# Attention rows mixed by 32 x 32 products before the value weights, and three row sums taken with the scores

## The chip, the cores and the metric

The kernel runs on one core of a Trainium2 chip. Its engines are TensorE (PE in the profile; its weight loads are listed apart as PEld), VectorE (DVE), ScalarE (ACT), GpSimd (POOL) and SyncE (SP, which issues DMAs). Each engine works through its own instructions in order. The metric is the device time of one execution in microseconds; lower is better.

## The reference

A graph of 10000 nodes with 160000 edges is propagated seven times; each node then has eight tokens (its own row and seven hops), on which one attention block and a weighted readout run:

```python
    h = x
    toks = [x]
    for _ in range(K):
        msg = h[src] * deg_inv_sqrt[src, None] * deg_inv_sqrt[dst, None]
        h = _segment_sum(msg, dst, N)
        toks.append(h)
    tok = jnp.stack(toks, axis=1)                      # (N, K+1, D)
    t = _layernorm(tok, axis=-1)
    q   = jnp.einsum('nkd,de->nke', t, wq)
    key = jnp.einsum('nkd,de->nke', t, wk)
    v   = jnp.einsum('nkd,de->nke', t, wv)
    scale = 1.0 / (D ** 0.5)
    attn = _softmax(jnp.einsum('nkd,nld->nkl', q, key) * scale, axis=-1)
    o = jnp.einsum('nkl,nld->nkd', attn, v)
    o = tok + jnp.einsum('nkd,de->nke', o, wo)
    r = _layernorm(o, axis=-1)
    alpha = _softmax(jnp.einsum('nkd,d->nk', r, w_r), axis=-1)
    return jnp.einsum('nk,nkd->nd', alpha, o)
```

K is 7, D is 128, everything is f32.

## The kernel before

The hops (`class Hops`) take the time up to 3300 us and are not touched. The change is in `attention` and in the constants that `Attention.constants` prepares.

**Tiling.** A group is 16 nodes x 8 tokens = 128 rows of 128 numbers. There are 625 groups, dealt into 40 supergroups: the first has one group, the other 39 have `SG` = 16. Within a group the 128 rows lie on the partitions, and each block of 32 partitions holds four whole nodes, so attention never crosses a block of 32.

**The steps for supergroup i**, by name. `xT` transposes the groups on PE, four to a PSUM bank (a "quarter"), and ScalarE copies them out. `uT` multiplies by `M`, which folds query and key weights, the centring and the scale. `val` multiplies each group by `Wv`, 131 columns: 128 for the value and output weights together, and three that yield one number per row each (column 128 feeds `extras`, 129 is the readout weight's product with the row, 130 is the row's difference of mean and first element, used by `norms`). `score` makes the 32 x 32 blocks of products in 32-column tiles of the array, and `soft1a`, `soft1b`, `soft_exp`, `soft2` pick each row's own eight numbers out of its block and take the softmax. `soft3` transposes the weights in 32 x 32 blocks on VectorE (`t4`), and four GpSimd copies put the blocks on the diagonal of `PT`, a 128 x 128 matrix per group that is zero elsewhere. `attend` multiplies `PT` with the values; `resid` adds the input on VectorE. `squares` (ScalarE, one activation per group with an accumulated sum) and `stats` (VectorE) give the second moments of the input and of the output; `norms`, `root`, `norms2` turn them into scales. `read1` to `read3` and `store` are the readout. `same_node` spreads numbers among the rows of a node by a product with a constant matrix (`sm`).

**Order.** The order is written out by hand: the loop at the end of `attention` runs over i, and each turn emits, for several supergroups at once, `xT` of i + 1, `val`, `uT` and `score` of i, softmax of i - 1, `attend` and `resid` of i - 2, `stats` of i - 3, and the readout of i - 4 and i - 5, in four parts q = 0 to 3. No planner moves anything; every engine executes its instructions in the order of the text. The tag `a` has three PSUM banks shared by `xT`, `uT` and `val`; `attend` has two of its own, `score` one, `sm` one, the readout one.

**In the profile** an f32 product appears as two loads and two products. The names there are those of tiles: `pt` and `xT` for `xT`, `pu` and `uT` for `uT`, `pv` and `v` for `val`, `po` for `attend`, `ps` for `score`, `pT` for the diagonal copies, `junk` for `squares`, `pf` for `read3`, `tab` for the input and output rows.

## Time and profile before

| what | value |
|---|---|
| median of three runs | 3979.82 us (3978.59 to 3985.85) |
| the profiled execution | 3981.58 us |
| its span, first to last instruction | 3979.8 us |
| mean granted TensorE clock | 0.972 |
| PE busy over the span | 3701.6 us (93%) |
| VectorE busy | 3304.5 us (83%) |
| ScalarE busy | 2650.2 us (67%) |
| GpSimd busy | 1682.8 us (42%) |
| first `pt` of the attention stage | 3304.93 us |

Shares over the whole span mix the hops with the attention stage, whose limits are others; the stage is the last 17% of the time, and its own rows have to be read by stretches. A group's row gives line, engine, operation, tiles (out <- in), shapes and count, then busy time and mean duration in ns, then the engine's idle time just ahead of these instructions and what ended it. In the views in order of time a row gives start, length and count of a run of like instructions; the ends of matmuls are modelled, so the distance between two starts is the surer measure.

### The profile page before, as it was taken

Reading aid. Unit: us, or ns where it says so; the run is one execution under the profiler, and the core shown is the slowest. Engines: PE = TensorE matmul, PEld = TensorE weight load, DVE = VectorE, ACT = ScalarE, POOL = GpSimd, SP = SyncE. Lnnn points to the kernel's source line nnn. Section 1 sums busy time; section 2 is a strip of 40 time slices with the busy share of each in tenths; the row PEclk is TensorE's granted clock in tenths of the full one; section 3 lists DMA queues with packets and bytes.
Section 4 is the critical chain, followed back from the end, with each engine's and each line's share of the span. In section 5 each row is a group of like instructions: output and inputs, shape, how many; then the busy total and the mean of one; then the engine's idle time right before and its main releaser. Section 6 shows DMA issues by size and latency. Waiting matters only on the chain. (4 is left out here: it accounts for less than half of the span.)

```text
span 3979.8 us, 163459 instructions
## 1 busy us (share of the span) xinstructions
PE 3701.6 (93%) x69691; PEld 3036.0 (76%) x69691; DVE 3304.5 (83%) x6945; ACT 2650.2 (67%) x6799; POOL 1682.8 (42%) x1900
## 2 busy tenths in 40 slices
PE   5776899999989999999999999999999998999997
PEld 3765666666657888888888888888888887888875
DVE  8999999999976777777777777777776666999998
ACT  6674366666665666666666666666665558888884
POOL 0000333333335555555555555555555552222222
PEclk8898899999989999999999999999999999999998
DMA  3100354444456666666666666666666662222220
GB/s 109 28 1 1 121 158 149 145 156 148 151 171 195 200 201 197 204 202 201 195 202 202 195 203 203 200 195 204 202 189 206 189 187 73 74 74 79 79 75 13
DMA packets 320616, 594.82 MB, mean 149 GB/s; under 512 B 55623, under 2 KB 213541, under 8 KB 314629
## 3 DMA queue, kind: packets, MB, share of 16 engines
q1 hardware_dynamic: 220005, 478.41, 38.6%
q0 software_dynamic: 35392, 72.55, 6.1%
q10 hardware_dynamic: 64480, 33.33, 2.9%
q8 instruction: 546, 8.95, 1.0%
q14 instruction: 193, 1.58, 0.1%
HBM read 455.43 MB, written 128.67 MB: 147 GB/s over the span
## 5 line engine op out<-in xcount | busy, mean ns | idle before, releaser
L545 ACT CAST eb<-p 128x512 f16<-128x512 f32 x3081 | 1591.3, 603 | 675.8 <-PE p L542 648.5
L545 DVE CAST eb<-p 128x512 f16<-128x512 f32 x1896 | 1179.4, 683 | 345.5 <-PE p L542 331.2
L542 PE MATMUL p<-tab,w 128*32 128x256 f16 x39816 | 1285.4, 274 | 34.7 <-ACT eb L545 23.0
L518 PE MATMUL acc<-eb,w 128*128 128x256 f16 (+1 forms) x9954 | 1238.9, 273 | 12.3 <-DVE indeg L593 9.7
L542 PEld LDWEIGHTS <-w 128*32 128x32 fp8e4 x39816 | 1002.0, 97 | 234.6 <-issue 181.9
L489 POOL DMA_INDIRECT og<-tabh,oidx x553 | 632.7, 1144 | 1257.0 <-PE acc L504 656.7
L518 PEld LDWEIGHTS <-w 128*128 128x128 fp8e4 x9954 | 952.6, 98 | 180.9 <-issue 68.7
L489 POOL DMA_INDIRECT og<-tabd,oidx x541 | 559.3, 1034 | 447.0 <-PE acc L531 265.4
L571 POOL TENSOR_SCALAR r<-s,ctok 128x128 f32<-128x128 f32 x474 | 296.8, 626 | 27.3 <-DVE s L533 13.4
L675 ACT ACTIVATE tab<-s,c 128x128 f16<-128x128 f32 x395 | 158.5, 401 | 202.8 <-DVE s L533 202.8
L676 DVE SCALAR_TENSOR_TENSOR tab<-s,c,tab 128x128 f16<-128x128 f32 x395 | 139.9, 354 | 183.1 <-ACT tab L675 183.0
L318 ACT ACTIVATE o<-oh,d2s 128x79 f16<-128x79 f16 x800 | 204.6, 372 | 79.3 <-PE ta L332 79.3
L533 DVE TENSOR_REDUCE s<-acc 128x128 f32<-128x256 f32 x553 | 228.5, 413 | 23.3 <-PE acc L531 16.1
L938 ACT ACTIVATE junk<-tab 128x128 f32<-128x128 f32 x625 | 245.1, 394 | 0.0
L479 DVE TENSOR_TENSOR w<-dsl,iof 128x2432 fp8e4<-128x2432 f16 x79 | 211.7, 2680 | 0.0
L332 PE MATMUL ta<-o,ro 128*128 128x158 f16 x1250 | 122.2, 270 | 76.9 <-DVE ro L328 76.9
L924 PEld LDWEIGHTS po<-v,pT 128*128 128x128 f32 x1250 | 159.0, 193 | 43.6 <-issue 27.6
L332 PEld LDWEIGHTS <-ro 128*128 128x128 f16 x1250 | 116.9, 115 | 81.3 <-DVE ro L328 81.1
L913 PE MATMUL pv<-Wv,xT 128*128 128x131 f32 x1250 | 175.3, 282 | 2.9 <-ACT xT L893 1.8
L996 POOL TENSOR_TENSOR p<-e,in 128x512 f32<-128x512 f32 (+1 forms) x40 | 40.8, 1019 | 322.3 <-DVE e L994 311.3
L924 PE MATMUL po<-v,pT 128*128 128x128 f32 x1250 | 166.6, 277 | 7.0 <-DVE tab L930 5.4
L913 PEld LDWEIGHTS pv<-Wv,xT 128*128 128x128 f32 x1250 | 152.2, 190 | 19.6 <-issue 8.2
(275 smaller groups left out, 4492.0 us busy)
## 6 DMA issues: line engine op xcount, KB each, us to landing
w<-gsd SPq DMA_DIRECT2D x474, 592.0 KB
gsd<-w SPq DMA_DIRECT2D x79, 592.0 KB
rb<-srow SPq DMA_DIRECT2D x79, 576.0 KB
tok<-r SPq DMA_DIRECT2D x546, 64.0 KB
tab<-tok SPq DMA_DIRECT2D x273, 128.0 KB
tabd<-tab ACTq DMA_DIRECT2D x395, 64.0 KB
og<-tabh,oidx POOLq DMA_INDIRECT x553
og<-tabd,oidx POOLq DMA_INDIRECT x541
```

The source lines that it names most:

```text
L318: A.activation(o[:, j - a, NK:, i], oh[:, j, :, i], AF.Copy, scale=d2s[:, ch, c0:c0 + 1])
L332: T.matmul(ta, ro[:, j - a, :, i], o[:, j - a, :, i], start=j + i == 0, stop=j + i == NP)
L479: V.tensor_tensor(w[:, :NJ * 128].rearrange("p (j d) -> p j d", d=128), dsl[:, g, :, None].to_broadcast([128, NJ, 128]), self.iof1[:, None ...
L489: self.nc.gpsimd.indirect_dma_start(out=o, out_offset=None, in_=src[0] if i == NI else src[1], in_offset=bass.IndirectOffsetOnAxis(ap=self ...
L518: T.matmul(acc[0][:, :m], w[:, J * 128:(J + 1) * 128], e[:, j, :m], start=first and J == 0, stop=J == NG - 1 and not (first or late))
L533: V.tensor_reduce(s, acc[0][:, 0:256].rearrange("p (h d) -> p d h", h=2), axis=X, op=ALU.add)
L542: T.matmul(p[32 * q:32 * q + 32, j], w[:, NJ * 128 + s * CAP:NJ * 128 + (s + 1) * CAP], tab[:, s, :], start=True, stop=True)
L545: (A.copy if evac(jj) else V.tensor_copy)(e[:, :n, 0:256], p[:, :n].rearrange("p j h d -> p j (h d)"))
L571: self.nc.gpsimd.tensor_scalar(r, s, ct[:, t:t + 1], None, op0=ALU.mult)
L913: T.matmul(p[:, g - a, :], S[i]["xT"][:, g, :], Wv, start=True, stop=True)
L924: T.matmul(p[:, g - a, :], PT[i % 2][:, g, :], S[i]["v"][:, g, :128], start=True, stop=True)
L938: A.activation(j, S[i]["x"][:, g, :], AF.Square, bias=S[i]["x"][:, g, 0:1], scale=-1.0, accum_out=S[i]["sq"][:, g:g + 1])
```

## The change

The rows are now weighted before they meet the value weights. `mix` multiplies, for each group and each block of 32 partitions, the block of the input (as the loaded operand, 32 partitions x 128 columns) by the transposed 32 x 32 block of softmax weights, in row tiles of the array, with one PSUM bank for each of the four blocks; four ScalarE copies bring the result, already transposed, to `yT`. `attend` then multiplies `yT` by `Wv`. `val`, its copies, `PT` and the GpSimd copies are gone. `score` changes sides: `xT` is loaded and `U` is streamed, which holds for each block of 32 columns of `uT` three columns of `Wv` behind it; the three numbers per row come out with the scores (64 numbers apart, two PSUM banks), and `sums` copies them. For the last two groups of a supergroup the second moments of the input come from VectorE (`xstats`, `NQ` = 14) in place of ScalarE, in one tile with those of the output. One PSUM tag of five banks serves `xT`, `uT`, `mix`, `attend` and `read3`. The order is written anew as one list.

```diff
-        T.matmul(pw[:, 0:128], wT[:, 0, :], wT[:, 1, :], start=True, stop=True)
+        T.matmul(pw[:, 0:128], wT[:, 1, :], wT[:, 0, :], start=True, stop=True)
...
+    U = cp.tile([128, SG, 4, 35], F32, name="U")
+    V.tensor_copy(U[:, :, :, 32:].rearrange("p g c e -> p (g c) e"), Wv[:, None, 128:].to_broadcast([128, 4 * SG, 3]))
...
+    def bank():
+        return pp.tile([128, 512], F32, name="a", tag="a", bufs=5)
...
+    def uT_copy(i, q):
+        a, b = quarter(i, q)
+        if a < b:
+            p = S[i].pop(("pu", q))[:, :(b - a) * 128]
+            A.copy(U[:, a:b, :, :32], p.rearrange("p (g c k) -> p g c k", c=4, k=32))
+
+    def mix(i):
+        n = sgs[i][1]
+        S[i]["yT"] = tp.tile([128, SG, 128], F32, name="yT")
+        p = S[i]["py"] = [bank() for _ in range(4)]
+        for g in range(n):
+            for c in range(4):
+                r = slice(32 * c, 32 * c + 32)
+                T.matmul(p[c][:, 32 * g:32 * g + 32], S[i]["x"][r, g, :], S[i]["t"][r, 32 * g:32 * g + 32],
+                         start=True, stop=True, tile_position=(32 * c, 0))
+
+    def mix_copy(i, c):
+        n = sgs[i][1]
+        A.copy(S[i]["yT"][:, :n, 32 * c:32 * c + 32], S[i]["py"][c][:, :32 * n].rearrange("p (g k) -> p g k", k=32))
...
-            T.matmul(p[:, g - a, :], PT[i % 2][:, g, :], S[i]["v"][:, g, :128], start=True, stop=True)
+                T.matmul(p[:, (g - a) * 128:(g - a + 1) * 128], S[i]["yT"][:, g, :], Wv[:, :128], start=True, stop=True)
...
-            for c in range(0, 128, 32):
-                T.matmul(p[c:c + 32, g, :], S[i]["uT", g // 8][:, g % 8, c:c + 32], S[i]["xT"][:, g, c:c + 32],
-                         start=True, stop=True, tile_position=(0, c))
+            for c in range(4):
+                T.matmul(p[32 * c:32 * c + 32, g, :35], S[i]["xT"][:, g, 32 * c:32 * c + 32], U[:, g, c, :],
+                         start=True, stop=True, tile_position=(0, 32 * c))
+
+    def sums(i):
+        n = sgs[i][1]
+        S[i]["y"] = sp.tile([128, SG, 11], F32, name="y")[:, :n]
+        A.copy(S[i]["y"][:, :, 8:], S[i]["s"][:, :n, 32:35])
...
-        for c in range(0, 128, 32):
-            G.tensor_copy(PT[i % 2][c:c + 32, :n, c:c + 32], t[c:c + 32, :n * 32].rearrange("p (g k) -> p g k", k=32))
...
+    def xstats(st, i):
+        for g in range(NQ, sgs[i][1]):
+            V.bn_stats(st[:, g - NQ, :], S[i]["x"][:, g, :])
...
+        do(score, i)
+        do(resid, i - 3, 3)
+        do(load, i + 3)
+        do(squares, i, 9, 12)
+        do(sums, i)
...
+        if ok(i - 3):
+            stats(st, i - 3, 0, 8)
+        do(squares, i, 12, NQ)
+        do(xT, i + 1, 0)
+        do(xT_copy, i + 1, 0)
+        do(soft1b, i - 1)
+        do(soft_exp, i - 1)
+        do(mix, i - 2)
+        do(soft1a, i)
+        for c in range(4):
+            do(mix_copy, i - 2, c)
+        do(soft2, i - 1)
+        do(soft2b, i - 1)
+        do(read1, i - 4)
+        do(read3, i - 5)
+        do(store, i - 5)
+        do(xT, i + 1, 1)
+        do(xT_copy, i + 1, 1)
+        do(uT, i + 1, 0)
+        do(uT_copy, i + 1, 0)
+        do(read_exp, i - 4)
+        if ok(i - 3):
+            stats(st, i - 3, 8, 12)
+        do(attend, i - 2, 0)
+        do(squares, i + 1, 0, 1)
+        do(resid, i - 2, 0)
+        do(xT, i + 1, 2)
+        do(xT_copy, i + 1, 2)
+        if ok(i - 3):
+            stats(st, i - 3, 12, 16)
+        if ok(i):
+            xstats(st, i)
+        do(uT, i + 1, 1)
+        do(uT_copy, i + 1, 1)
+        do(squares, i + 1, 1, 3)
+        do(xT, i + 1, 3)
+        do(xT_copy, i + 1, 3)
+        do(attend, i - 2, 1)
+        do(squares, i + 1, 3, 4)
+        do(resid, i - 2, 1)
+        v = norms(i, i - 3, st)
+        do(uT, i + 1, 2)
+        do(uT_copy, i + 1, 2)
+        y = root(v)
+        do(soft3, i - 1)
+        do(read2, i - 4)
+        do(squares, i + 1, 4, 6)
+        do(uT, i + 1, 3)
+        do(uT_copy, i + 1, 3)
+        do(attend, i - 2, 2)
+        norms2(i, i - 3, v, y)
+        do(squares, i + 1, 6, 9)
+        do(attend, i - 2, 3)
+        do(resid, i - 2, 2)
```

## The prediction

> **What bounds the kernel now.** I read the page first, then busy time in stretches of the attention stage (it begins at 3304.9 us, where the first `pt` runs, and ends with the span), then the chain that ended last, then the list of waits, then one period of each engine in order of time. The columns of the first view are stretch, length, busy us of PE, weight loads, VectorE, ScalarE and GpSimd with their instruction counts, granted clock, DMA share and GB/s.

> ```profile
> 3600.00:3700.00 100.00, 98.86 (x1613) 81.14 (x1613) 95.29 (x337) 88.56 (x329) 26.20 (x43) 1.00 0.28 80
> ```

> The scores in the chain (start, length, engine, tile, line, count), first and last of 26 such rows:

> ```profile
> 3464.18 1.24 PE ps L944 x82
> ...
> 3868.68 1.24 PE ps L944 x82
> ```

> And PE's only row in the waits of 3500 to 3800 us (total, times, longest):

> ```profile
> PE pt L892 <- PE ps L944: 3.6, 18, 0.2
> ```

> 25 periods take 404.50 us, 16.18 us each. PE is busy 98.9% at full clock, VectorE 95.3%. PE waits 0.2 us per period, for its own scores; VectorE is not in that list at all. So two engines run without a pause, both for the whole period, and ScalarE has about 1.9 us of air (88.6%). A change must shorten both to help, and the smaller gain counts.

> **What goes from PE.** One period in order of time (start, length, engine, line, op, tile, shape, count; the distance of two starts is what a group costs):

> ```profile
> 3609.47 1.30 PE L944 MATMUL ps<-xT,uT 128*32 128x32 f32 x128
> 3610.94 0.63 PE L892 MATMUL pt<-ident,tab 128*128 128x128 f32 x4 [0.17 <-PE ps L944]
> 3611.40 0.84 PE L913 MATMUL pv<-Wv,xT 128*128 128x131 f32 x6
> 3612.17 0.64 PE L950 MATMUL sm<-rb,same 128*32 128x256 f32 x8
> 3612.62 0.66 PE L950 MATMUL sm<-lb,same 128*32 128x128 f32 x8
> 3613.21 0.94 PE L913 MATMUL pv<-Wv,xT 128*128 128x131 f32 x6
> 3614.08 1.08 PE L1092 MATMUL pf<-tab,Ab 128*32 128x128 f32 x32
> 3615.09 0.94 PE L913 MATMUL pv<-Wv,xT 128*128 128x131 f32 x6
> 3615.86 1.05 PE L924 MATMUL po<-v,pT 128*128 128x128 f32 x8
> 3616.75 0.60 PE L892 MATMUL pt<-ident,tab 128*128 128x128 f32 x4
> 3617.19 1.73 PE L913 MATMUL pv<-Wv,xT 128*128 128x131 f32 x14
> 3618.76 0.61 PE L924 MATMUL po<-v,pT 128*128 128x128 f32 x4
> ```

> The value products (L913) take 0.77 + 0.87 + 0.77 + 1.57 = 3.98 us of a period, the changes to and from 32-column tiles around `sm` and `pf` among it. They go. `xT`, `uT`, `attend`, `sm` and `pf` keep their counts; the scores stream 35 columns for 32 at 128 products in 1.30 us, and I take nothing for that (at most 35/32, 0.1 us). Two or three changes of tiling come back at 0.1 us each. PE without `mix` is 16.12 - 3.98 + 0.25 = 12.4 us (this period was 16.12 to its neighbour before).

> **What `mix` costs** is not in the trace: nothing loads 32 partitions by 128 columns. Per period it is 16 x 4 products, each in two passes as every f32 product here (`ps`: 64 written, 128 recorded), so 128 loads and 128 products of 32 columns. The nearest rows (loads and scores over 300 us: count, busy us, mean ns):

> ```profile
> L913 PEld LDWEIGHTS pv<-Wv,xT 128*128 128x128 f32 x602 | 72.9, 190 | 7.5 <-issue 3.8 <-ACT junk L938 3.8
> L892 PEld LDWEIGHTS pt<-ident,tab 128*128 128x128 f32 x296 | 33.9, 141 | 5.0 <-PE ps L944 5.0
> L944 PEld LDWEIGHTS ps<-xT,uT 128*32 128x32 f32 x2304 | 21.3, 109 | 2.2
> ```

> A score loads a quarter of the array (128 x 32), streams 32 columns, and goes four tiles side by side: 1.30 us for 128, 10 ns each, though one load alone lasts 109 ns. A `mix` product loads the other kind of quarter (32 x 128), streams the same 32 columns, is issued as often and in the same order of tiles. That is the nearest row: 1.30 us, 1.4 with its change of tiling. By columns instead: 190 against 109 ns for 96 columns more is 0.84 ns a column, 108 ns for 128, and with four row tiles side by side 32 x 0.108 = 3.5 us; that `pt` loads the same 128 x 128 in 141 ns says that columns alone don't set it, and by that row a load of 128 columns holds its tile for 27 (32 columns at 0.84) + 141 - 109 = 59 ns, and `mix` is 32 x 0.059 = 1.9 us. With nothing side by side, 128 x 0.108 = 13.8 us. The low end is 0.9 (each tile's 32 loads at 27 ns). I take 1.4, and keep 0.9 to 13.8. [...]

> **VectorE.** Four copies on GpSimd (L1012) go, since `mix` reads the transposed rows where they are. They stand beside six small operations:

> ```profile
> 3622.76 2.55 POOL L1012 COPY pT<-t 32x512 f32<-32x512 f32 x4 [3.04 <-DVE rx L1028]
> 3622.80 0.59 DVE L1029 SCALAR_TENSOR_TENSOR rv<-sq,rx 128x16 f32<-128x16 f32 x1
> 3623.32 0.17 DVE L1034 TENSOR_TENSOR rd<-st 128x16 f32<-128x16 f32 x1
> 3625.25 0.27 DVE L1077 TENSOR_REDUCE rz<-re 128x16 f32<-128x128 f32 x1
> ...
> 3319.58 0.18 DVE L1029 SCALAR_TENSOR_TENSOR rv<-sq,rx 128x16 f32<-128x16 f32 x1 [0.21 <-ACT junk L938]
> 3319.79 0.18 DVE L1038 TENSOR_SCALAR rv<-rv 128x32 f32<-128x32 f32 x1
> ...
> 3965.73 0.19 DVE L1034 TENSOR_TENSOR rd<-st 128x16 f32<-128x16 f32 x1
> 3966.55 0.28 DVE L1077 TENSOR_REDUCE rz<-re 128x16 f32<-128x128 f32 x1
> ...
> 3619.78 1.64 DVE L1019 BATCH_NORM_STATS2 st<-tab 128x6 f32<-128x128 f32 x8
> 3621.33 0.67 DVE L930 TENSOR_TENSOR tab<-po,tab 128x512 f32<-128x512 f32 x1
> ```

> From L1034 to L1077 it is 1.93 us beside the copies and 0.82 in the tail, with GpSimd idle; L1029 has 0.52 to its successor beside them and 0.21 at the start. So 1.11 + 0.31 = 1.42 us go. Two statistics of x come (L1019: 8 in 1.55 us): 0.39. Other operations are reordered, not added; those on 18 columns for 16 change nothing that shows. VectorE: 16.12 - 1.42 + 0.39 = 15.1 us.

> **ScalarE.** Two squares and the value copies go, four `mix` copies of the size of `uT`'s come.

> ```profile
> L938 ACT ACTIVATE junk<-tab 128x128 f32<-128x128 f32 x297 | 116.4, 393 | 0.0
> L914 ACT COPY v<-pv 128x393 f32<-128x393 f32 x94 | 45.4, 483 | 14.1 <-PE pv L913 11.2
> L903 ACT COPY uT<-pu 128x512 f32<-128x512 f32 x74 | 42.8, 578 | 5.3 <-PE pu L902 5.0
> ```

> Five long value copies a period: -2 x 0.39 - 5 x 0.48 + 4 x 0.58 = -0.9 (a short sixth value copy and the copy of `y` go and the three sums come, all small; I set them against each other). 88.6% of 16.18 is 14.3; 13.4 remain, so ScalarE doesn't bound. That the rows of `U` are 35 apart I price at nothing; what covers it is 1.7 us of ScalarE's air below VectorE's 15.1.

> **The new loop.** In the new order each period hangs together thus: the second `attend` quarter on PE, its residual, the norms, the two root activations, two squares, the last `uT` copy, then the next scores, which need all of `U` (one buffer). PE from the scores to the end of that quarter: 1.47 + 1.04 (`sm`) + 0.46 + `mix` + 0.15 + 1.01 (`pf`) + 3 x 0.44 (`pt`) + 2 x 0.86 (`pu`) + 2 x 0.89 (`po`) = 8.95 + `mix`. Behind it: 0.2 to drain, 0.67, norms 0.25 + 0.21 + 0.82, roots 0.5, squares 0.78, copy 0.58, about 4.0 in all (`pu` is four passes in 1.72 us; roots by these rows).

> ```profile
> 3606.76 1.88 PE L902 MATMUL pu<-xT,M 128*128 128x512 f32 x4
> 3608.48 1.05 PE L924 MATMUL po<-v,pT 128*128 128x128 f32 x8
> ...
> 3625.53 0.24 ACT L1044 ACTIVATE ry<-rv 128x32 f32<-128x32 f32 x1
> 3625.80 0.23 ACT L1045 ACTIVATE ry<-ry 128x32 f32<-128x32 f32 x1
> ```

> That is 13.0 + `mix`: 14.4 at 1.4, hidden below VectorE's 15.1 until `mix` passes 2.1 us. The five shared PSUM banks, of which `mix` takes four at once, I cost at nothing: each is freed by a copy that stands ahead of its next user, with 1 us of `pf` between; without that cover the first `pt` behind it waits some 0.6 us, still inside the loop.

> **The sum.** The period becomes VectorE's 15.1, 1.07 less than 16.18. Full periods begin with the scores of supergroup 4 and end with those of the last, 39; the rows are of 4 and 38:

> ```profile
> 3367.12 1.30 PE L944 MATMUL ps<-xT,uT 128*32 128x32 f32 x128
> ...
> 3917.16 1.30 PE L944 MATMUL ps<-xT,uT 128*32 128x32 f32 x128
> ```

> That is 34 periods and one more, 35 x 1.07 = 37.5 us. In the shorter periods at the head PE or ScalarE leads, and one period of the tail loses the copies: 2 to 4 us more; `mix`, its copies and `attend` in a row cost about as much in the last two periods, where nothing covers them. 3981.6 (the profiled execution; its span is 3979.8) - 37.5 = 3944. The runs' median is 1.8 below that execution, less than what I can resolve.

> **The rivals.**
> 1. **Loads side by side, but by columns** (other side). Place: `mix`; price 3.5 to 3.9 us; it decides from 3.2 us on, where 13.0 + `mix` passes 16.18. The period is 16.5 to 16.9, 35 times 0.35 to 0.75: 3994 to 4008. For it: 109 against 190 ns; against it: 141 ns, and 10 ns per score. [...]
> 2. **Row tiles load two at a time or one after another**: 6.9 or 13.8 us, periods of 19.9 or 26.8, 4112 or 4353 us. Against it: the four column tiles of the scores overlap.
> 3. **`mix` between 3.0 and 3.4 us**: within 0.2% of before.
> 4. **The change doesn't do what it says on VectorE**: the six operations stay long for another reason. VectorE has 16.5, and the time is 3993. Against it: the tail, where they are short with GpSimd idle.

> **How the numbers follow.** Forecast 0.62 (its own range 3925 to 3960: VectorE from 14.7, if more of its operations lose company, to 15.6 with waits), rival 1 0.16, rival 2 0.12, rival 3 0.06, rival 4 0.04. The range 3925 to 4010 leaves out rival 2 and edges. 0.2% (8 us) is about what a measurement of this kernel can tell from no change. Faster 0.64, same 0.08, slower 0.28.

> **What would show it.** The period between scores at 15.1; VectorE with no entry in the waits and PE with some; L1034 to L1077's successors at 0.2 us each; `mix` at 1.3 to 2 us from first load to the next group. A `mix` of 3.5 us with ScalarE waiting for it and PE waiting for the last `uT` copy proves rival 1; 7 or more, rival 2.

## The result and the profile after

| | median | lowest to highest | profiled execution | mean granted clock |
|---|---|---|---|---|
| before | 3982.55 us | 3978.59 to 3985.85 (4 runs) | 3981.58 us | 0.972 |
| after | 4071.24 us | 4065.92 to 4078.97 (4 runs) | 4070.35 us | 0.951 |

The change makes the kernel slower: the ratio of the times is 1.0225, with an interval from 1.0213 to 1.0237. The forecast was 3944, with a range that ended at 4010.

Busy time in two stretches of the attention stage of the kernel after (stretch, length, busy us of PE, weight loads, VectorE, ScalarE and GpSimd with their counts, granted clock, DMA share, GB/s):

```profile
3500.00:3600.00 100.00, 98.55 (x2086) 78.93 (x2085) 79.17 (x309) 71.42 (x260) 9.96 (x17) 0.88 0.23 66
3600.00:3700.00 100.00, 98.61 (x1871) 78.66 (x1868) 76.20 (x300) 72.06 (x251) 10.21 (x16) 0.86 0.25 70
```

Two things differ from before. VectorE has fallen from 95% to 76 to 79%, so it no longer sets the period. PE is as full as it was, but its granted clock is 0.87 here and was 1.00. The scores of supergroups 5 and 39 in the view of PE in order of time give the period (35 scores between and with them):

```profile
3372.32 1.27 PE L959 MATMUL ps<-U,xT 128*32 128x35 f32 x126
...
4000.82 1.30 PE L959 MATMUL ps<-U,xT 128*32 128x35 f32 x128
```

34 periods take 628.5 us, 18.49 us each, against 16.18 before. 35 x 2.31 = 81 of the 88.8 us between the two profiled executions; the head and the tail hold the rest.

Now PE inside one of these periods, one of the shorter ones with 17.62 us (start, length, engine, line, operation, tiles, shape, count; what one group costs is the distance of two starts):

```profile
3631.45 1.31 PE L959 MATMUL ps<-U,xT 128*32 128x35 f32 x128
3632.95 0.64 PE L971 MATMUL sm<-rb,same 128*32 128x256 f32 x8 [0.20 <-DVE rb L978]
...
3634.33 3.88 PE L925 MATMUL a<-t,tab 32*128 32x32 f32 x128
3638.14 1.94 PE L1115 MATMUL a<-tab,Ab 128*32 128x128 f32 x32
3640.01 1.12 PE L898 MATMUL a<-ident,tab 128*128 128x128 f32 x4
```

`mix` (L925) lasts from 3634.33 to 3638.14, 3.81 us, where the forecast had 1.4. And the 32 products of `read3` behind it (L1115) last 1.87 us, where the same group took 1.01 before. The granted clock in narrow stretches around these rows says why `read3` is slow:

```profile
3634.30:3636.30 2.00, 2.00 (x73) 1.97 (x72) 1.93 (x10) 1.00 (x5) 0.00 (x0) 1.00 0.26 66
3636.30:3638.10 1.80, 1.80 (x67) 1.77 (x63) 1.70 (x5) 0.31 (x1) 0.00 (x0) 0.93 0.80 250
3638.10:3640.10 2.00, 2.00 (x37) 1.48 (x34) 1.83 (x9) 1.90 (x4) 0.80 (x1) 0.50 0.68 172
3640.10:3642.00 1.90, 1.90 (x7) 1.38 (x8) 1.10 (x6) 1.09 (x4) 0.23 (x1) 0.69 0.34 99
3642.00:3645.00 3.00, 3.00 (x23) 2.47 (x22) 1.86 (x7) 2.44 (x7) 0.00 (x0) 1.00 0.13 36
```

The clock is whole while nearly all of this `mix` runs, drops to half at its end, and comes back after some 3.4 us. In stretches of 0.4 us from 3635.00 on it is 1.00 up to 3637.80, 0.50 in all seven from 3638.20 to 3641.00, and 1.00 again from 3641.40; with only these two values, 0.07 x 1.8 x 2 + 2.0 + 0.31 x 1.9 x 2 = 3.4. PE is "busy" throughout: the second column of each row is the same number as the first. Nothing in PE's busy time gives this away, only the clock does.

The period ahead of it fares worse: its `mix` (from 3614.39) lasts 5.57 us, the cut begins inside it, and the four stretches from 3615.70 to 3624.30 stand at 0.87, 0.50, 0.50 and 0.52, by the same working 6.8 us at half, twice as long. From 3360 to 4000 us, again in stretches of 0.4 us and by this working, the clock drops 34 times, once a period: 20 times for 3.4 us, 14 times for 6.8, and nowhere below 0.50. Where the clock is whole from end to end (3541.40 to 3545.10) `mix` lasts 3.70 us. Over the stage the clock is 0.87, and 0.13 of 18.49 us is 2.4 us; without it the period would be 16.1 by this estimate, the period of before.

So there are two suspects: a `mix` that is 2.3 to 2.4 us longer than forecast, and a clock that is cut behind it or already inside it. The experiments take them apart.

### The profile page after: what moved, and what is told of

It reads as the page before. It is cut to its first block, busy times and chain, and to the rows that moved or that the text cites. A ratio compares the mean times of both kernels' runs of the same rounds, so it can differ in the third digit from the quotient of the medians.

```text
span 4068.6 us, 170729 instructions
## 1 busy us (share of the span) xinstructions
PE 3787.4 (93%) x73441; PEld 3093.2 (76%) x73441; DVE 3265.6 (80%) x7036; ACT 2611.4 (64%) x6568; POOL 1584.3 (39%) x1738
## 4 chain that ended last, share of the span: by engine, by line
PE 62%; DVE 5%; DMA 1%; ACT 1%; issue 1%; ACTq 0%; POOL 0%; SPq 0%; DVEq 0%; POOLq 0%
PE p L542 23%; PE acc L518 22%; PE a L925 4%; PE acc L504 4%; PE a L898 2%; PE a L909 2%; PE a L939 2%; PE a L1115 2%; PE sm L971 1%; DVE tab L945 1%; DMA og<-tabh,oidx 1%; DVE t L1028 1%; DMA tabd<-tab 0%; ACT junk L953 0%; DVE l L1076 0%
## 5 line engine op out<-in xcount | busy, mean ns | idle before, releaser
L945 DVE TENSOR_TENSOR tab<-a,tab 128x512 f32<-128x512 f32 (+1 forms) x157 | 104.2, 684 | 136.9 <-PE a L939 136.9
L953 ACT ACTIVATE junk<-tab 128x128 f32<-128x128 f32 x547 | 213.7, 393 | 0.0
L939 PEld LDWEIGHTS a<-Wv,yT 128*128 128x128 f32 x1250 | 168.2, 206 | 49.6 <-issue 25.8
L909 PE MATMUL a<-xT,M 128*128 128x512 f32 (+1 forms) x314 | 178.4, 672 | 4.2 <-ACT xT L903 4.2
L1106 POOL TENSOR_TENSOR Ab<-sel,rz 128x128 f32<-128x128 f32 (+1 forms) x79 | 31.2, 414 | 371.0 <-DVE rz L880 356.1
L939 PE MATMUL a<-Wv,yT 128*128 128x128 f32 x1250 | 169.2, 287 | 0.8 <-ACT yT L930 0.8
```

The costliest lines, as they stand in the source:

```text
L909: T.matmul(p[:, :(b - a) * 128], M, S[i]["xT"][:, a:b, :], start=True, stop=True)
L939: T.matmul(p[:, (g - a) * 128:(g - a + 1) * 128], S[i]["yT"][:, g, :], Wv[:, :128], start=True, stop=True)
L953: A.activation(j, S[i]["x"][:, g, :], AF.Square, bias=S[i]["x"][:, g, 0:1], scale=-1.0, accum_out=S[i]["sq"][:, g:g + 1])
```

## The experiments

The theory: a `mix` product loads 128 columns and streams only 32; the loads set its time, and a long run of such thin streams is what the clock is cut for. Against it: row tiles as such are slow or cut the clock, or the new order hangs in a loop (the first rival's last `uT` copy).

**The stream made wide.** Each product streams all of 128 columns behind the same load; what a product writes beside its own columns is overwritten or left, so the values in `yT` are partly others.

```diff
-                T.matmul(p[c][:, 32 * g:32 * g + 32], S[i]["x"][r, g, :], S[i]["t"][r, 32 * g:32 * g + 32],
+                w = min(128, 32 * n)
+                k = min(32 * g, 32 * n - w)
+                T.matmul(p[c][:, k:k + w], S[i]["x"][r, g, :], S[i]["t"][r, k:k + w],
```

> The changed kernel, but each mix product streams 128 columns of the transposed weights in place of 32 (neighbouring columns are overwritten, so yT holds sums of the wrong columns); loads, order, copies are the same. Theory A (the granted clock is cut because mix streams little while it loads much; mix itself is as long as its loads): mix stays at 3.7 to 3.9 us, the granted clock of the stage returns from 0.87 to 0.97 or more, the period falls from about 18.5 to 16.4-16.8 us, the time to 3990-4010 us. Theory B (row tiles or their loads cut the clock whatever they stream): clock stays near 0.87, time 4065-4085 us. Theory C (mix's 32-column stream, not the load, sets its length): mix grows beyond 5 us and the time beyond 4110 us.

3993.83 us (3992.52 to 3999.49), 1.0041 of before [1.0026, 1.0056]: four times the streamed columns, and 77 us faster than after. The same stretch, and one period of PE:

```profile
3600.00:3700.00 100.00, 98.19 (x2198) 78.55 (x2199) 87.09 (x343) 78.71 (x287) 11.01 (x18) 1.00 0.27 74
```

```profile
3613.72 1.31 PE L961 MATMUL ps<-U,xT 128*32 128x35 f32 x128
...
3616.61 3.85 PE L927 MATMUL a<-t,tab 32*128 32x128 f32 x128
3620.39 1.08 PE L1117 MATMUL a<-tab,Ab 128*32 128x128 f32 x32
...
3629.87 1.31 PE L961 MATMUL ps<-U,xT 128*32 128x35 f32 x128
```

The clock is 1.00, `mix` lasts 3.78 us (3616.61 to 3620.39), against 3.70 with 32 columns at whole clock, and this period is 16.15. Not every period is as short: the 34 from the scores at 3366.43 to those at 3924.86 average 16.42, because some runs of `mix` last longer, up to 4.82 us; in or just behind some of them PE is seen to stop for up to 0.78 us with no engine to wait for. Four times the stream costs next to nothing beside the load (0.08 us of `mix`), and with this change alone the clock is 1.00 in each of the five stretches of 100 us from 3400 to 3900, where after has 0.85 to 0.88: it is the thin stream that goes with the cut.

**One load for four groups.** The wide stream again, with one product per block for four groups: 32 loads instead of 128. The rows of the other three groups are weighted with the first group's input, so three quarters of `mix` are left out.

```diff
-        for g in range(n):
+        for g in range(0, n, 4):
...
-                T.matmul(p[c][:, 32 * g:32 * g + 32], S[i]["x"][r, g, :], S[i]["t"][r, 32 * g:32 * g + 32],
+                w = min(128, 32 * n)
+                T.matmul(p[c][:, 32 * g:32 * g + w], S[i]["x"][r, g, :], S[i]["t"][r, 32 * g:32 * g + w],
```

> The changed kernel with a quarter of the mix loads: the block of one group in four is loaded and streams the weights of all four groups (the other three groups' rows are left out of the sum). 32 loads and products of 128 columns in place of 128 of 32. If loads side by side by columns set mix's length, it takes 32/4 x 0.116 = 0.93 us, the clock stays at 1.00, and the period is then VectorE's, which I put at 15.1 us in the prediction: 3940-3950 us. If VectorE's sum was wrong too (or the loop through the roots and the last uT copy binds), the period is 15.6 us or more and the time over 3960 us.

3940.02 us (3935.28 to 3942.80), 0.9898 [0.9883, 0.9913]. Its `mix`, and the stretch:

```profile
3611.12 1.30 PE L960 MATMUL ps<-U,xT 128*32 128x35 f32 x128
...
3614.00 1.34 PE L926 MATMUL a<-t,tab 32*128 32x128 f32 x32
3615.27 1.08 PE L1116 MATMUL a<-tab,Ab 128*32 128x128 f32 x32
3617.41 0.66 PE L898 MATMUL a<-ident,tab 128*128 128x128 f32 x4 [1.06 <-ACT yT L931]
```

```profile
3600.00:3700.00 100.00, 92.13 (x1669) 67.65 (x1663) 94.90 (x375) 85.57 (x308) 12.05 (x19) 1.00 0.30 85
```

With `mix` at 1.27 us the next scores start at 3626.25, a period of 15.1 (14.97 on average over 34, 3371.81 to 3880.87), VectorE is at 95% and waits for no engine, and PE has time to wait. That is the forecast's case (`mix` 1.4, period 15.1, 3944 us) and its time to 4 us. The price of the first suspect is 3993.83 - 3940.02 = 54 us, with the longer periods of the wide run, some 34 x (16.42 - 16.15) = 9 us, counted in.

**Between 32 and 128 columns.** Streams of 64 columns, first with the neighbour's columns left in `yT`:

```diff
+                w = min(64, 32 * n)
+                k = min(32 * g, 32 * n - w)
+                T.matmul(p[c][:, k:k + w], S[i]["x"][r, g, :], S[i]["t"][r, k:k + w],
```

> As e1_wide, but each mix product streams 64 columns: between the changed kernel (32: clock 0.87, 4071 us) and e1_wide (128: clock 1.00, 3994 us). The loads are the same, so mix is 3.7 to 3.9 us where the clock is full. If the clock follows how much is streamed in proportion, the clock of the stage is 0.91 to 0.95 and the time 4015-4050 us; if there is a threshold, it is one of the two ends: 4060-4080 us (64 is still too little) or 3985-4005 us (64 is enough).

3998.59 us (3996.65 to 4006.61), 1.0038 [1.0022, 1.0053], clock 1.00, `mix` 3.73 us. Then in the full computation, each product writing its own 32 columns and 32 more that the next product overwrites:

```diff
-                T.matmul(p[c][:, 32 * g:32 * g + 32], S[i]["x"][r, g, :], S[i]["t"][r, 32 * g:32 * g + 32],
+                w = min(64, 32 * (n - g))
+                T.matmul(p[c][:, 32 * g:32 * g + w], S[i]["x"][r, g, :], S[i]["t"][r, 32 * g:32 * g + w],
```

> The changed kernel with each mix product streaming 64 columns, its own 32 and the next group's, whose place the next product then overwrites with the right sums; the result is that of the reference. By e4_64 a stream of 64 keeps the clock at 1.00 and costs nothing beside the loads: mix 3.7 us, time 3990-4008 us, as e4_64. If the order of the overwriting makes products of one bank wait for each other, mix is longer than 4.5 us and the time over 4030 us.

3997.05 us (3990.43 to 4006.55), 1.0043 [1.0028, 1.0057]. PE's row and the next, then two stretches:

```profile
3615.59 3.77 PE L926 MATMUL a<-t,tab 32*128 32x64 f32 x128
3619.29 1.08 PE L1116 MATMUL a<-tab,Ab 128*32 128x128 f32 x32
```

```profile
3500.00:3600.00 100.00, 98.25 (x2196) 78.83 (x2200) 87.74 (x343) 79.64 (x294) 11.04 (x18) 1.00 0.26 74
3600.00:3700.00 100.00, 98.11 (x2148) 78.64 (x2144) 84.81 (x333) 76.79 (x277) 11.04 (x18) 0.97 0.26 74
```

Useless columns win back 74 of the 89 us. Of the five stretches of 100 us from 3400 to 3900 only the second one above is below 1.00 (0.97); it holds a period of 20.22 us, from 3660.89, in whose `mix` PE also stopped for 0.52 us. With the neighbour's columns left in `yT` the clock is 1.00 in the three stretches from 3500 to 3800. No run has a `mix` that streams more than 32 columns and fewer than 64.

**The row tiles undone alone.** The blocks go back on the diagonal of a 128 x 128 matrix, by four GpSimd copies as before the change, and `mix` becomes 16 full products (32 with their two passes); all else stays as after.

```diff
-            for c in range(4):
-                r = slice(32 * c, 32 * c + 32)
-                T.matmul(p[c][:, 32 * g:32 * g + 32], S[i]["x"][r, g, :], S[i]["t"][r, 32 * g:32 * g + 32],
-                         start=True, stop=True, tile_position=(32 * c, 0))
+            T.matmul(p[g // 4][:, g % 4 * 128:g % 4 * 128 + 128], S[i]["x"][:, g, :], PT[i % 2][:, g, :], start=True, stop=True)
...
+        for c in range(0, 128, 32):
+            G.tensor_copy(PT[i % 2][c:c + 32, :n, c:c + 32], t[c:c + 32, :n * 32].rearrange("p (g k) -> p g k", k=32))
```

> The changed kernel with only the row tiles undone: the block-diagonal matrix and its four GpSimd copies are back, and mix is 16 full products of 128x128 (loads the rows, streams the diagonal matrix) in two passes. By theory A mix takes 32 x 0.111 = 3.55 us, nearly what the row tiles take at full clock (3.70), and the clock is 0.97 or more, so the two seconds lost to the clock come back although nothing is tiled: period 16.2 to 16.7 us by PE (VectorE 16.5 with the copies beside it again), time 3985-4005 us. If the loss is the new order's (banks, loop) and not the clock's, the period stays over 17.5 us and the time over 4030 us.

4031.16 us (4025.12 to 4035.52), 1.0125 [1.0109, 1.0140], clock 1.00. On PE, and what runs on GpSimd and VectorE just ahead of it:

```profile
3603.47 0.64 PE L973 MATMUL sm<-rb,same 128*32 128x256 f32 x8 [1.65 <-DVE rb L980]
3604.75 3.74 PE L927 MATMUL a<-pT,tab 128*128 128x128 f32 x32
3608.41 1.08 PE L1119 MATMUL a<-tab,Ab 128*32 128x128 f32 x32
```

```profile
3599.69 2.55 POOL L1032 COPY pT<-t 32x512 f32<-32x512 f32 x4 [6.29 <-PE a L941]
```

```profile
3601.01 0.61 DVE L886 SCALAR_TENSOR_TENSOR ry<-rz,ry 128x32 f32<-128x32 f32 x1
3601.66 0.60 DVE L1080 TENSOR_TENSOR l<-w,ry 128x16 f32<-128x16 f32 x1
```

32 full loads take 3.66 us and 128 quarter loads 3.7 to 3.8: four row tiles side by side carry about what one load of the whole array does. The time is over what was expected for another reason, a wait that comes back with the copies: they stand beside the last operations of the norms, the two shown last 0.6 us each instead of 0.28 and 0.32 after, `rb` is late, and PE waits for it for 1.65 us in each period. In the kernel after, with the transposition in the same place and no copies, that wait is 0.20 us.

**The same with the copies elsewhere.** The transposition and its copies are emitted ahead of the next statistics, which read one tensor only.

```diff
+        do(soft3, i - 1)
...
-        do(soft3, i - 1)
```

> e3_diag (row tiles undone, full clock, 4031 us, same_node waiting 1.9 us a period for rows that VectorE writes late) with soft3 moved ahead of the third statistics, so that the four GpSimd copies stand beside statistics and not beside the norms' last operations. If that wait is all that e3_diag had too much, the period falls from 17.7 to 15.9-16.3 us and the time to 3970-3990 us, level with before, with mix still 3.7 us. If not, it stays over 4010 us.

3963.51 us (3961.97 to 3964.79), 0.9944 [0.9928, 0.9961]: 0.6% faster than before and, by the two ratios, 2.7% faster than after. The stretch, and one period:

```profile
3500.00:3600.00 100.00, 100.00 (x1658) 81.93 (x1657) 91.77 (x360) 84.11 (x295) 27.41 (x45) 1.00 0.30 84
```

```profile
3604.74 1.27 PE L961 MATMUL ps<-U,xT 128*32 128x35 f32 x126
...
3607.12 3.74 PE L927 MATMUL a<-pT,tab 128*128 128x128 f32 x32
3610.78 1.08 PE L1119 MATMUL a<-tab,Ab 128*32 128x128 f32 x32
...
3620.26 1.27 PE L961 MATMUL ps<-U,xT 128*32 128x35 f32 x126
```

No wait for another engine is left on PE, which works the whole of this period of 15.5 us at full clock (15.63 on average over 34). With full products in place of the 32 x 32 ones and the copies in this place, the rest of the change is worth 21 us (before, in the same comparison, 3984.40).

**Is it the thin stream or the row tile?** From the last kernel, each full product cut into four, each with its own load of 128 x 128 and 32 streamed columns; no row tiles anywhere.

```diff
-            T.matmul(p[g // 4][:, g % 4 * 128:g % 4 * 128 + 128], S[i]["x"][:, g, :], PT[i % 2][:, g, :], start=True, stop=True)
+            for c in range(0, 128, 32):
+                T.matmul(p[g // 4][:, g % 4 * 128 + c:g % 4 * 128 + c + 32], S[i]["x"][:, g, :], PT[i % 2][:, g, c:c + 32], start=True, stop=True)
```

> e6_diag2 (full products, no row tiles, full clock, 3964 us) with each product of 128 streamed columns cut into four of 32, each with its own load of 128x128: the same sums, four times the loads, nothing tiled. By loads alone mix is 128 x 0.108 = 13.8 us at full clock, the period 25.7 us, the time about 4330 us. If a thin stream is what cuts the clock, it is cut here too: clock of the stage below 0.85, mix 18-28 us, time over 4450 us. If the cut belongs to row tiles, the clock stays at 0.97 or more and the time is 4310-4360 us.

One execution, 5052.35 us; on the chip that ran it the kernel before took 4214.46 us, slower in the hops, so only rows of the attention stage are compared.

```profile
3600.00:3700.00 100.00, 100.00 (x957) 90.84 (x955) 41.25 (x166) 38.46 (x134) 11.43 (x18) 0.70 0.11 33
```

```profile
3611.45 22.45 PE L928 MATMUL a<-pT,tab 128*128 128x32 f32 x128
```

The clock is 0.70 with PE busy 100.00 of 100 us, where the last kernel has 1.00 in 3500 to 3600 us. The clock of the full array is cut as well when it streams 32 columns for 128 loaded: the row tile isn't the cause.

**The order of the tiles.** After, with the two loops of `mix` exchanged, so that 16 groups of one block follow each other.

```diff
-        for g in range(n):
-            for c in range(4):
+        for c in range(4):
+            for g in range(n):
```

> The changed kernel with mix's two loops exchanged: all 16 groups of one block of 32 partitions first, then the next block, so that neighbours in the order share a row tile; same loads, products and result. If row tiles go side by side only when neighbours in the order use different ones, mix is 128 x 0.11 = 14 us, periods near 27 us and the time about 4400 us. If PE looks far enough ahead to mix the blocks anyway (a block is 64 instructions), mix stays near 4 us and the time near 4070 us.

One execution, 4764.05 us, clock about 0.7 in the stage. One `mix`, the row behind it and the next `mix`:

```profile
3592.15 21.82 PE L925 MATMUL a<-t,tab 32*128 32x32 f32 x128
3613.91 1.94 PE L1115 MATMUL a<-tab,Ab 128*32 128x128 f32 x32
...
3628.98 21.28 PE L925 MATMUL a<-t,tab 32*128 32x32 f32 x128
```

21.76 us instead of 3.81, 170 ns a product instead of 30, at a clock of 0.70 and 0.68 in the two stretches of 100 us from 3500 to 3700. From this `mix` to the next it is 36.83 us, of which 0.69 is 25.4; less the 12.4 of a period without `mix` (16.15 - 3.78 with the wide stream) it would be some 13 us at full clock by this estimate. Neighbours in the order that use the same tile no longer go side by side, and the clock, 0.86 to 0.88 after in these stretches, falls further with the longer run of thin streams. This is near the second rival's price (13.8 us, and the clock on top), and it shows that in the change the four tiles did overlap.

**`mix` in two halves**, with `read3` between, so that no thin run is longer than 1.9 us:

```diff
-        do(mix, i - 2)
+        do(mix, i - 2, 0)
+        do(read3, i - 5)
+        do(mix, i - 2, 1)
```

> The changed kernel, all of its work, with mix in two halves of eight groups and read3 (1.0 us of 128-column products) between them. The copies still wait for the second half, so the first xT products behind it now wait some 0.6 us more for a PSUM bank. If the clock is cut because one stretch of about 3.4 us is nearly all mix, two stretches of 1.9 us with dense work between should keep part of it: clock 0.92 or more, time 4010-4050 us. If it is cut by the total amount of thin work in a period, or one microsecond between is too short, clock and time stay: 0.85-0.88, 4065-4095 us.

4051.72 us (4050.38 to 4057.79), 1.0171 [1.0153, 1.0189], a little over what was expected. The clock is at 0.95 to 1.00 in stretches of 100 us from 3400 to 3900, but every period has a new wait (17 times in 300 us, 10.6 us); one of them:

```profile
3640.57 1.31 PE L961 MATMUL ps<-U,xT 128*32 128x35 f32 x128
...
3646.39 1.99 PE L927 MATMUL a<-t,tab 32*128 32x32 f32 x64
3649.04 0.66 PE L898 MATMUL a<-ident,tab 128*128 128x128 f32 x4 [0.66 <-ACT yT L932]
...
3657.72 1.30 PE L961 MATMUL ps<-U,xT 128*32 128x35 f32 x128
```

The next `xT` follows the second half directly, and waits 0.66 us for a copy to `yT` to free its bank. With more changes of tiling this undisturbed period is 17.15 (3640.57 to 3657.72), and the mean of 34 is 17.69. The forecast had said that without `read3` behind `mix` this wait would be some 0.6 us.

**Smaller loads.** Each product in two of 64 loaded columns (32 x 64 tiles, 256 loads):

```diff
+                for h in (0, 64):
+                    T.matmul(p[c][h:h + 64, 32 * g:32 * g + 32], S[i]["x"][r, g, h:h + 64], S[i]["t"][r, 32 * g:32 * g + 32],
+                             start=True, stop=True, tile_position=(32 * c, h))
```

> The changed kernel with each mix product cut into two of 64 loaded columns (tiles of 32 rows and 64 columns): twice the loads and products, 256 a period, each load half as wide, all work done. If a load's time is its columns (0.84 ns each) and eight tiles go side by side, 32 x 0.054 = 1.7 us would do and the issue of 256 pairs at 10 ns sets 2.6 us; the products of 32 columns then come closer together and the clock is cut less (0.9 or more): 3960-4020 us. If the two halves of a row block do not load side by side, mix stays at 3.7 us or more with the clock at 0.87: 4060-4090 us. If a load costs the same however few columns it has, mix is 7.4 us and the time over 4180 us.

4182.78 us (4179.33 to 4185.73), 1.0507 [1.0486, 1.0528]. One `mix`:

```profile
3634.71 1.52 PE L926 MATMUL a<-t,tab 32*64 32x32 f32 x124
3638.47 2.04 PE L926 MATMUL a<-t,tab 32*64 32x32 f32 x128 [2.25 <-issue]
3642.77 0.43 PE L926 MATMUL a<-t,tab 32*64 32x32 f32 x4 [2.25 <-issue]
```

And the stretch:

```profile
3600.00:3700.00 100.00, 84.53 (x2072) 64.59 (x2067) 62.80 (x248) 61.97 (x217) 7.87 (x14) 0.81 0.19 53
```

The time lies where the third expectation had it, for another reason. A burst runs at 1.52 / 124 = 12 ns per product, so 256 would take 3.1 us; but between bursts PE stands still for 2.25 us and the view names no engine as the cause ("issue"). The stops are 128 recorded products apart, with their loads 256 instructions; no run shows what sets them. The clock, expected at 0.9 or more, is 0.81. The products stream 32 columns for 64 loaded here, but PE also stands still for 4.5 us of this `mix`, so this run doesn't tell with which of the two the clock falls.

**The kernel before, with VectorE relieved.** Two runs ask whether VectorE or PE set the old period. In the first only `soft3` moves ahead of the second statistics:

```diff
+            if q == 1 and ok(i - 1):
+                soft3(i - 1)
...
-            if q == 1 and ok(i - 1):
-                soft3(i - 1)
```

> The kernel before with one call moved: soft3 (the 32x32 transposes and the four GpSimd copies behind them) stands ahead of the second eight statistics in place of behind them, so that the copies run beside statistics and not beside the small operations of the norms. VectorE's sum falls by about 1.1 us of 16.1, nothing else changes. If PE alone would still need the whole period (my reading that both engines are full), the time stays within 0.2% of before (period 16.0 to 16.2). If VectorE alone set the period, it falls by up to 1.1 us x 35 = 38 us, to about 3942 us.

3977.27 us (3972.68 to 3980.72), 0.9991 [0.9982, 1.0000].

```profile
3600.00:3700.00 100.00, 98.86 (x1614) 81.22 (x1613) 86.33 (x335) 89.96 (x328) 26.17 (x43) 1.00 0.28 80
```

VectorE falls from 95.3 to 86.3% and PE stays at 98.86: PE alone fills the period. In the second, `same_node` and `read3` also stand right behind the scores, so that the groups in 32-column tiles follow each other, and the roots one place earlier:

```diff
+        sm = pp.tile([128, 4, SG * 8], F32, name="sm", tag="m", bufs=1).rearrange("p a (g k) -> p a g k", k=8)
...
+            same_node(sm[:, 0:2, :m], S[i - 1]["rb"][:, :, :m])
...
+            read3(i - 5)
...
-                if c == 3:
+                if c == 2:
```

> The kernel before with soft3 moved as in b1_soft3, and on PE the same_node products and read3 put right behind the scores, so that all 32-column tiles stand in one run and four of six changes of tiling go (0.1 to 0.2 us each, about 0.4 us a period); the roots go ahead of the last two uT products so that same_node's rows are ready. If PE alone sets the period, it falls from 16.18 to 15.6-15.9 us: 3955-3972 us. If same_node then waits for its rows on VectorE (0.5 us or more), nothing is won: 3975-3990 us.

3987.25 us (3983.22 to 3989.40), 1.0003 [0.9994, 1.0012]; the wait for `same_node`'s input didn't come, but another did:

```profile
3602.31 0.64 PE L1092 MATMUL pf<-tab,Ab 128*32 128x128 f32 x14 [1.26 <-issue]
```

PE stops for 1.26 us within a run of narrow instructions that no other engine holds up, as in the kernel with smaller loads; the next stop, at 3619.45, comes 254 recorded products later, with their loads 508 instructions, where the kernel with smaller loads has 256. Undisturbed periods are 15.93 us (scores at 3500.62 and 3516.55), but 34 average 16.37, and the stops take back what the fewer tile changes save.

## Why the prediction was wrong

**What bounds the kernel** was right for PE and half right for VectorE. Both had no pause, but relieving VectorE alone gives next to nothing (ratio 0.9991, upper end 1.0000), so the change had to shorten PE.

**What goes from PE** was right: the value products are gone, and PE's other groups keep their costs (scores to `sm` 1.50 us, `read3` 1.01 at full clock).

**"What `mix` costs"** is the first step that failed. Taken: 1.4 us from the scores' 10 ns per product; measured: 3.70 us where the clock is whole, 3.81 in the period shown, and 3.70 to 3.78 with wider streams. The scores load 32 columns into each tile, 108 ns a load after, and `mix` loads 128. Its own loads, beside the full ones of `attend` in 3500 to 3800 us (count, busy us, mean ns):

```profile
L925 PEld LDWEIGHTS a<-t,tab 32*128 32x128 f32 x2092 | 66.1, 198 | 3.9 <-issue 3.9
L939 PEld LDWEIGHTS a<-Wv,yT 128*128 128x128 f32 x521 | 68.1, 200 | 20.4 <-issue 12.0 <-ACT xT L903 4.7 <-PE a L909 3.8
```

A quarter of the rows, the same duration (187 ns in 3541.40 to 3545.10 us and 192 in 3624.60 to 3634.20, where the clock is whole). So the score was not the nearest row: the load of 32 rows x 128 columns lasted as long as that of 128 x 128, not as long as that of 128 x 32. The forecast's own sum by columns, 3.5 us, which it set aside for `pt`'s 141 ns, was 0.2 to 0.3 too low; the same transposes load in 140 ns after (3624.60 to 3634.20), and no run shows why. With a `mix` as short as forecast the time is 3940; its real length brings it to 3994, the 54 us above. Four tiles at a time made a quarter-row load as cheap as a full one over four, no cheaper: 3.70 us for 128 of them, 3.66 us for the 32 full products without row tiles. The products saved (3.98 us with their tile changes) and the products added are nearly the same work, and PE, which is the bound, has nothing left: the forecast's 12.4 us without `mix` and 3.78 make 16.2, and 16.15 were measured in an undisturbed period with the clock whole (16.42 on average, with the longer ones), against 16.18 before.

**The missing term** is the second failure, and the larger: no step asked what clock the new mixture of instructions would be granted. By the three runs with wider streams (3994 to 3999 us) it costs 73 to 77 us, out of the 89 between before and after. The trace of after shows the drops (to 0.50, for 3.4 or 6.8 us as worked out above), with PE 98.6% busy over 3600 to 3700 us, so PE's busy time does not tell them. In stretches of 100 us the clock is 0.85 to 0.88 with 32 columns streamed per 128 loaded in row tiles as after, 0.70 with 32 per 128 on the full array, 0.97 to 1.00 with 64, 1.00 with 128. That the drop goes with thin streams is shown by these runs; what grants the clock is not.

**VectorE** was right. The five small operations that stood beside the copies, from the first of them to what follows the last, on VectorE in order of time after:

```profile
3646.58 0.18 DVE L1056 TENSOR_TENSOR rd<-st 128x18 f32<-128x18 f32 x1
...
3647.41 0.70 DVE L1028 STREAM_TRANSPOSE t<-p 128x512 f32<-128x512 f32 x1
```

They take 0.83 us; the forecast had 0.82, and 1.93 stood before.
With a short `mix` VectorE's period is 15.0 and the time 3940; 15.1 and 3944 were summed. The fourth rival (operations that stay long) is out.

**ScalarE** was right: 72% after, 86% with the short `mix`, never the bound.

**The new loop** did not decide. The rows show no wait of PE for the last `uT` copy; PE's only entries in the waits of 3500 to 3800 us after are (total, times, longest):

```profile
PE sm L971 <- DVE rb L978: 3.5, 17, 0.2
PE a L925 <- issue: 0.4, 1, 0.4
```

**The PSUM banks**, taken at nothing, cost nothing after, where the list above has no wait for them. In the forecast's own case they do: with one load for four groups PE waits some 1.1 us in each period for ScalarE's copies of `mix`, `read3` between them or not (22.0 us in 20 waits). VectorE's longer period hides it.

So **the first rival** had the right price of the loads (3.5 to 3.9 us) and, without the clock, the right time (3994 to 4008; 3994 and 3997 measured), but its mechanism was not the one at work: PE is full, with undisturbed periods of 16.15, where the loop would have made them 16.5 to 16.9 with PE waiting. What lifted the mean to 16.42 are the longer runs of `mix` and PE's own stops, which no rival has; that the time agrees is luck. **The second rival**'s price was neared only with the tiles in another order (some 13 us at full clock by the estimate above). Both, and the forecast, lacked the clock, and that is why the range ended 61 us short.

## What to carry to other kernels

Before a product in row tiles is priced by the nearest row of a trace, compare the columns that the two load: here the row with 32 loaded columns gave 1.4 us, and 128 loads of 32 x 128 with the four tiles in turn took 3.70, as long as 32 loads of 128 x 128 (3.66). Fewer loads helped here (`mix` 1.27 us with 32 of 32 x 128); narrower ones ran faster in bursts (12 ns per product), but the stops between the bursts took more than that (4.5 us in one `mix`). Read the granted clock in stretches of 2 us, not only the busy share: here the clock stood at 0.50 for 3.4 us behind 3.7 us that streamed 32 columns per 128 loaded, and streaming columns that nobody needs won back 74 us. Take the period from many scores, not from one pair. The GpSimd copies and their transposition cost this kernel 68 us less beside the statistics than beside the small operations of the norms (3963.51 against 4031.16), so look at what stands beside them.
